# Rows of the value tile 144 bytes apart instead of 132, so that every row begins on 16 bytes

## Chip, cores and metric

One core of one Trainium2 chip. The metric is the device time of one execution in microseconds (us). Six executions of this kernel lay between 427.55 and 428.86 us, 0.3% apart, so the change discussed here is read mostly from the traces: the hardware's own record of when each instruction started.

## The reference

Grouped-query attention (8 batches, 16 query heads over 4 key/value heads, 384 positions, head size 64), followed by a feed-forward layer with a squared ReLU.

```python
def _attn_ref(q, k, v):                       # q [8,16,384,64], k and v [8,4,384,64]
    k = np.repeat(k, group, axis=1); v = np.repeat(v, group, axis=1)
    scores = scale * np.matmul(q, k.transpose(0, 1, 3, 2))
    attn = np.exp(scores - np.max(scores, axis=-1, keepdims=True))
    attn = attn / (np.sum(attn, axis=-1, keepdims=True) + 1e-09)
    return np.matmul(attn, v)

def _moe_ref(x, w_in, w_out):                 # x [3072,1024], w_in [1024,2048], w_out [2048,1024]
    h = np.maximum(x @ w_in, 0.0)
    return h * h @ w_out
```

## The kernel before

The kernel keeps both weight matrices in on-chip memory (SBUF) and interleaves, on the tensor engine (PE), the attention of one batch with the feed-forward matmuls of an earlier one. Only one piece of it matters here. The values of a batch lie in a tile `v_aug` of 12 rows per partition (4 heads x 3 blocks of 128 positions). A row holds 64 values and a 1.0, so that one matmul gives both the weighted sum and the denominator of the softmax. It reads 65 of the 66 elements of a row: 130 of 132 bytes.

```python
    DP = D + 2                                                     # 66
    v_st  = [sb(f"v_st{i}", [128, NU, D]) for i in range(NST)]     # NU = 12 rows
    v_aug = [sb(f"v_aug{i}", [128, NU, DP]) for i in range(2)]     # batches take turns
    ...
    def aug_v(b, eng):                                             # on POOL
        R.add(eng, lambda e: e.tensor_copy(v_aug[b % 2][:, :, 0:D], v_st[b % NST][:, :, :]), ...)
    ...
    def av(b, c, banks):
        g, s2 = c // 2, c % 2
        i = pick(banks)
        po = bank(i)[:, 0:2 * NJ * DP].rearrange("p (f e) -> p f e", f=2 * NJ)
        def mm(pe, f0):
            for f in range(f0, f0 + NJ):
                for j in range(NJ):                                # NJ = 3 rows are accumulated
                    w = expT[:, (b * NU + g * NJ + j) % NEX, f % 2, (f // 2) * 128:(f // 2) * 128 + 128]
                    m = pe.matmul(po[:, f - 6 * s2, 0:D + 1], w, v_aug[b % 2][:, g * NJ + j, 0:D + 1],
                                  start=(j == 0), stop=(j == NJ - 1))
            return m
    ...                                        # reciprocal of column D, multiply, store as bf16
    for i in range(2):
        R.add("vector", lambda e, i=i: e.memset(v_aug[i][:, :, D:D + 1], 1.0), writes=[("v_one", i)])
```

So within a head `g` the matmuls read rows 3g, 3g+1, 3g+2, then jump back to 3g, 3g+1, 3g+2 and so on, six times per `av`. In all there are 1,152 such matmuls, mostly in bursts of 36. Each is preceded by its own weight load (1,152 LDWEIGHTS on the same line in the page below).

The softmax here doesn't subtract the row's maximum and nothing guards it: scores larger than these inputs give would overflow.

Of the kernel before, what the change touches and what calls it, by code (L numbers as in the profile page):

```python
# [139 lines left out]
def bass_gqa_attention__then__ffn_squared_relu_kernel(  # L140
# [11 lines left out]
    B, H, S, D = 8, 16, 384, 64  # L152
# [6 lines left out]
    NU = HKV * NJ  # L159
    UC = 4 * S  # L160
    HC = UC // 2
    DP = D + 2
    NST, NEX, NXT, NHR, NY = 2, 8, 3, 4, 3

    R = Recorder(nc)
# [1 line left out]
    def sb(name, shape, dt=bf16):  # L167
        return nc.alloc_sbuf_tensor(name, shape, dt)
# [5 lines left out]
    q_f32 = sb("q_f32", [128, 4, NJ * D], f32)  # L174
    k_dup = [sb(f"k_dup{i}", [128, NU, 2, D]) for i in range(2)]
    v_st = [sb(f"v_st{i}", [128, NU, D]) for i in range(NST)]
    v_aug = [sb(f"v_aug{i}", [128, NU, DP]) for i in range(2)]
    kT = [sb(f"kT{i}", [128, NU, 128]) for i in range(2)]
    qT = [sb(f"qT{i}", [128, 2 * NU, 128]) for i in range(2)]
    expT = sb("expT", [128, NEX, 2, HC])  # L180
# [11 lines left out]
    def bank(i):  # L192
        return ps[:, i, :]
# [4 lines left out]
    def pick(allowed):  # L198
        turn_count[0] += 1
        i = min(allowed, key=lambda i: (max(R.when(writes=[("bank", i)]), R.clock["tensor"]), used[i]))  # L200
        used[i] = turn_count[0]
        return i
# [171 lines left out]
# [5 lines that stand above are left out]
# [387 lines left out]
```

## Time and profile before

| | before |
|---|---|
| time, median | 427.7 us (427.55 to 427.76, 3 runs) |
| span of the profiled run | 426.2 us |
| PE busy | 420.4 us, 99% |
| the 1,152 attention-times-value matmuls on the chain that ended last | 8.3% of the span |
| their mean start to start, inside bursts | 31.2 ns |

The page of the kernel before: first the busy time of each engine, then the chain of work that ended last (share of the span by engine), then the two groups of line 383, PE matmuls and weight loads (busy us, mean ns of one, then idle time of the engine just before them).

```profile
PE 420.4 (99%) x3435; PEld 232.0 (54%) x3464; DVE 157.9 (37%) x332; ACT 194.8 (46%) x194; POOL 55.4 (13%) x68
...
PE 96%; DMA 1%; issue 1%; ACT 1%; POOL 1%; DVE 0%; POOLq 0%
...
L383 PEld LDWEIGHTS ps<-v_aug,expT 128*128 128x128 bf16 x1152 | 40.0, 97 | 6.9 <-issue 0.6
L383 PE MATMUL ps<-v_aug,expT 128*128 128x65 bf16 x1152 | 42.0, 193 | 0.0
```

PE is the bound, and it is bound by its own stream of matmuls, not by waits. Who PE waited for, in the same kernel (total us, times, longest):

```profile
PE ps L555 <- PEq L751: 0.8, 1, 0.8
PE ps L496 <- issue: 0.5, 3, 0.2
PE ps L311 <- DMA q_st<-in_q_dram: 0.4, 1, 0.4
PE ps L337 <- ACT expT L347: 0.2, 1, 0.2
```

These sum to 1.9 us. The mean of 193 ns in the group is the length of one record, whose end the profiler models; the records overlap, since their starts lie 31.2 ns apart. What counts is the distance between starts, called the interval or pitch below. The timeline of the kernel before shows it for three bursts (start us, length us, engine, line, how many):

```profile
240.28 1.26 PE L383 MATMUL ps<-v_aug,expT 128*128 128x65 bf16 x36
251.34 1.28 PE L383 MATMUL ps<-v_aug,expT 128*128 128x65 bf16 x36
257.87 1.28 PE L383 MATMUL ps<-v_aug,expT 128*128 128x65 bf16 x36
```

A burst of 1.28 us is 35 intervals and one length of 0.193 us: (1.28 - 0.193)/35 = 31.1 ns. The individual records give each interval to the nanosecond. Two bursts' beginnings, batch 5 (rows 0, 1, 2) and batch 4 (rows 3, 4, 5), in ns from each start to the next:

```
batch 5, rows 0 1 2:  29 35 32 | 30 32 33 | 29 33 33 | 29 32 33 | 29 32 32 | 29 34 32
batch 4, rows 3 4 5:  29 29 36 | 29 29 34 | 29 29 33 | 30 29 33 | 29 29 34 | 29 29 33
```

An interval is counted to the row read by the matmul at whose start it begins. It differs by row.

### The profile page before, as it was taken

How to read it: one execution, taken by the hardware profiler on the slowest of the kernel's cores; microseconds unless marked ns; L12 is line 12 of the kernel's file. 1: busy time of each engine (PE TensorE's matmuls, PEld its weight loads, DVE VectorE, ACT ScalarE, POOL GpSimd, SP SyncE). 2: the span in 40 equal slices, each digit the busy share in tenths (PEclk: the TensorE clock that was granted, in tenths of full speed). 3: DMA queues.
4: the chain of work that ended last, by engine and by line, in shares of the span. 5: the costliest groups of instructions: out<-in, count | busy, mean ns of one | idle time of the engine just before them, and what ended most of it. 6: DMA issues, size and time to landing. Idle time of an engine off the chain costs nothing.

```text
span 426.2 us, 7813 instructions
## 1 busy us (share of the span) xinstructions
PE 420.4 (99%) x3435; PEld 232.0 (54%) x3464; DVE 157.9 (37%) x332; ACT 194.8 (46%) x194; POOL 55.4 (13%) x68
## 2 busy tenths in 40 slices
PE   8999999999999999999999999999999999999997
PEld 6565554555545555455554455544564465446544
DVE  3664431343424443144442344422441244114412
ACT  6957730477355773547745377552240033003300
POOL 8680001234013004003100000000000000000000
DMA  9999999999789178938918321033001100110012
GB/s 177 184 184 200 186 201 226 180 158 158 145 182 167 26 106 125 149 94 134 120 45 180 92 34 25 12 88 102 25 2 49 74 26 2 49 74 26 1 67 82
DMA packets 96915, 44.30 MB, mean 104 GB/s; under 512 B 77296, under 2 KB 90864, under 8 KB 96880
## 3 DMA queue, kind: packets, MB, share of 16 engines
q0 software_dynamic: 36544, 17.44, 32.1%
q1 hardware_dynamic: 59664, 25.86, 28.7%
q8 instruction: 27, 0.44, 0.4%
q10 hardware_dynamic: 672, 0.49, 0.4%
q14 instruction: 8, 0.07, 0.1%
HBM read 35.65 MB, written 12.58 MB: 113 GB/s over the span
## 4 chain that ended last, share of the span: by engine, by line
PE 96%; DMA 1%; issue 1%; ACT 1%; POOL 1%; DVE 0%; POOLq 0%
PE ps L440 40%; PE ps L496 39%; PE ps L383 8%; PE ps L358 7%; DMA q_st<-in_q_dram 1%; PE ps L337 1%; ACT expT L347 1%; PE ps L311 0%; PE ps L416 0%; POOL q_st L239 0%; PE ps L294 0%; POOL v_st L232 0%; DVE qT L318 0%; DVE y_sb L505 0%; POOL ident L523 0%
## 5 line engine op out<-in xcount | busy, mean ns | idle before, releaser
L440 PE MATMUL ps<-xT,w_in_sb 128*128 128x384 bf16 x1024 | 174.8, 326 | 0.0
L496 PE MATMUL ps<-w_out_sb,h2T 128*128 128x512 bf16 (+2 forms) x755 | 167.5, 375 | 1.9 <-issue 0.5
L368 ACT ACTIVATE expT<-ps 128x3072 bf16<-128x3072 f32 x42 | 114.5, 2727 | 64.8 <-PE ps L358 64.0
L440 PEld LDWEIGHTS ps<-xT,w_in_sb 128*128 128x128 bf16 x1024 | 97.0, 98 | 69.6 <-issue 6.8
L450 ACT ACTIVATE h2T<-hr 128x384 bf16<-128x384 f32 x128 | 64.5, 520 | 140.9 <-DVE hr L448 140.9
L496 PEld LDWEIGHTS ps<-w_out_sb,h2T 128*128 128x128 bf16 x784 | 73.8, 98 | 87.1 <-issue 5.1
L448 DVE TENSOR_SCALAR hr<-ps 128x384 f32<-128x384 f32 x128 | 71.2, 557 | 106.4 <-PE ps L440 106.4
L505 DVE COPY y_sb<-ps 128x512 f32<-128x512 f32 (+2 forms) x49 | 33.4, 681 | 122.8 <-PE ps L496 122.8
L383 PEld LDWEIGHTS ps<-v_aug,expT 128*128 128x128 bf16 x1152 | 40.0, 97 | 6.9 <-issue 0.6
L383 PE MATMUL ps<-v_aug,expT 128*128 128x65 bf16 x1152 | 42.0, 193 | 0.0
L398 DVE TENSOR_TENSOR o_sb<-ps,rinv 128x384 bf16<-128x384 f32 x64 | 35.7, 558 | 2.2
L358 PE MATMUL ps<-qT,kT 64*128 64x512 bf16 (+1 forms) x336 | 34.6, 325 | 0.0
L358 PEld LDWEIGHTS ps<-qT,kT 64*128 64x128 bf16 x336 | 13.0, 94 | 20.7 <-issue 6.3
L392 DVE RECIPROCAL rinv<-ps 128x6 f32<-128x6 f32 x64 | 12.2, 190 | 27.3 <-PE ps L383 27.3
L271 POOL COPY v_aug<-v_st 128x768 bf16<-128x768 bf16 x8 | 6.6, 831 | 83.9 <-PE ps L383 68.4
L347 ACT ACTIVATE expT<-ps 128x1024 bf16<-128x1024 f32 (+1 forms) x20 | 16.9, 980 | 1.1 <-PE ps L337 0.8
L266 POOL COPY k_dup<-k_st 128x1536 bf16<-128x1536 bf16 x7 | 10.3, 1470 | 43.5 <-DMA k_st<-in_k_dram 43.5
L239 POOL DMA_DIRECT2D q_st<-in_q_dram x17 | 14.8, 883 | 0.9 <-POOLq L751 0.8
L207 POOL DMA_DIRECT2D k_st<-in_k_dram x7 | 5.3, 757 | 39.4 <-DMA qT<-q_st 39.4
L337 PE MATMUL ps<-qT,kT 64*128 64x384 bf16 (+2 forms) x48 | 7.5, 343 | 0.3 <-ACT expT L347 0.2
L249 POOL DMA_DIRECT2D w_in_sb<-in_moe_w_in_dram x8 | 7.1, 891 | 0.0
L232 POOL DMA_DIRECT2D v_st<-in_v_dram x8 | 6.3, 784 | 0.1
(26 smaller groups left out, 41.9 us busy)
## 6 DMA issues: line engine op xcount, KB each, us to landing
out_dram<-y_sb SPq DMA_DIRECT2D x47, 256.0 KB, 2.0
q_st<-in_q_dram POOLq DMA_DIRECT2D x14, 384.0 KB, 8.2
w_in_sb<-in_moe_w_in_dram POOLq DMA_DIRECT2D x8, 512.0 KB, 14.5
w_out_sb<-in_moe_w_out_dram POOLq DMA_DIRECT2D x4, 1024.0 KB, 30.8
v_st<-in_v_dram POOLq DMA_DIRECT2D x8, 192.0 KB, 9.8
k_st<-in_k_dram POOLq DMA_DIRECT2D x7, 192.0 KB, 4.4
q_st<-in_q_dram POOLq DMA_DIRECT2D x3, 192.0 KB, 5.4
xT<-o_sb SPq DMA_TRANSPOSE x28, 3.1
```

Of the source, the lines that this page charges most:

```text
L239: R.add("gpsimd", lambda g: g.dma_start(q_st[st][:, h0:h1, :], q[b, h0:h1].rearrange("h (p j) d -> p h (j d)", j=NJ)), writes=[("q_st", st ...
L347: R.add("scalar", lambda e: e.activation(dst, src, AF.Exp, scale=0.125), reads=keys, writes=[("expT", (b * NU + u) % NEX, t) for u, _, _ i ...
L358: m = pe.matmul(flat[:, k0 * HC + c0:k0 * HC + c1], kT[b % 2][64 * x:64 * x + 64, u + k0, :], q_cols(b, (u + k0) // NJ, x, c0, c1))
L368: R.add("scalar", lambda e: e.activation(dst, src, AF.Exp, scale=0.125), reads=keys, writes=[("expT", (n + m) % NEX, t) for m in range(2) ...
L383: m = pe.matmul(po[:, f - 6 * s2, 0:D + 1], w, v_aug[b % 2][:, g * NJ + j, 0:D + 1], start=(j == 0), stop=(j == NJ - 1))
L392: R.add("vector", lambda e: e.reciprocal(rinv[r].ap().unsqueeze(2), po[:, :, D:D + 1]), reads=[("bank", i)], writes=[("rinv", r)], cost=0.13)
L398: R.add("vector", lambda e: e.tensor_tensor(dst, srcv, rbv, ALU.mult), reads=[("bank", i), ("rinv", r)], writes=[("o_sb", o, s2)], cost=0.48)
L440: m = pe.matmul(bank(i)[:, 0:S], w_in_sb[:, kc, c * 128:(c + 1) * 128], xT[b % NXT][:, kc, :], start=(kc == 0), stop=(kc == NKC - 1))
L448: R.add("vector", lambda e: e.tensor_scalar_max(hr[r][:, :], bank(i)[:, 0:S], 0.0), reads=[("bank", i)], writes=[("hr", r)], cost=0.48)
L450: R.add("scalar", lambda e: e.activation(h2T[b % 2][:, c, :], hr[r][:, :], AF.Square), reads=[("hr", r)], writes=[("h2T", b % 2, c)], cost ...
L496: m = pe.matmul(bank(i)[:, 0:n], h2T[b % 2][:, c, i3 * 128:(i3 + 1) * 128], w_out_sb[:, c, c0:c1], start=(c == 0), stop=(c == NFC - 1))
L505: R.add("vector", lambda e: e.tensor_copy(ysl, bank(i)[:, 0:n]), reads=[("bank", i)], writes=[("y", yb)], cost=0.08 + n / 960)
```

## The change

The intent: with rows 132 bytes apart, three rows in four begin off a multiple of 16 bytes. At 144 bytes every row begins on one.

```diff
-    DP = D + 2
+    DP, DV = D + 2, D + 8
@@
-    v_aug = [sb(f"v_aug{i}", [128, NU, DP]) for i in range(2)]
+    v_aug = [sb(f"v_aug{i}", [128, NU, DV]) for i in range(2)]
```

The layout (`DP`) in PSUM, the memory that matmuls write into, stays. Both value tiles start on 64 bytes before and after, and all later tensors move by 256 bytes. The order of instructions on every engine is the same in both kernels.

## The prediction

> **What bounds the kernel.** The tensor engine. Busy row of the page: PE 420.4 us of a span of 426.2 (99%). The chain of waits that ended last is 96% PE; its attention-times-value matmuls (line 383, 128x65) hold 8%, about 35 us. The wait table gives PE 1.9 us of idle.
>
> **What the change does.** Same instructions, order and PSUM layout. Value rows start 144 instead of 132 bytes apart, so all start on 16 bytes. Before, both value tiles start on a multiple of 64 bytes and take 1,600 with padding; they will take 1,728, so later tensors move by 256 bytes and keep their alignment. Only the value copy on POOL (8 x 831 ns, off the chain), two 68 ns fills, and the 1,152 matmuls see the new spacing.
>
> **Cost, read from the single matmul records.** Start to start inside the bursts is 31.2 ns on average, but depends on the row that is read. Rows 0 and 8: 29.2. Rows 1, 2, 5, 7, 10, 11: 31.9 to 33.6. Row 4 (16-aligned): 29.2. But misalignment itself costs nothing: rows 3 and 9 (offsets 12 and 4 within 16 bytes) run at 29.5 and 29.1, and rows 3, 6 and 9 take 29 straight after a feed-forward matmul. What slow rows share is the junction: the last of the 65 elements of the row before lies in the 16-byte piece in which the new row starts. Where a row starts on 16 bytes, or the matmul jumps back two rows, the piece is another and the pitch is 29. The exception is row 6 after row 8: 31.3 although the pieces differ; there row 8's last piece holds a single element.
>
> [...] this trace shows 29.2 in the fast cases, 162.8 for 384 columns.
>
> After the change no junction shares a line. Best: all 1,152 at 29.2, saving 1,152 x 2.0 ns = 2.3 us. Against it: every row then ends with one element alone in its line, like row 8. If a third of the matmuls (the jumps back) then cost 31.3, the mean is 29.9 and the gain 1.5 us; if all do, nothing is gained. PE almost never waits, so nearly all reaches the end; in the first 26 us, where exp on ACT paces PE, up to 0.3 us may be lost.
>
> **Predicted:** 425.8 us (-0.4%), 8 in 10 between 425.0 and 427.4. Faster by over 2%: 0.01; within 2%: 0.98; slower: 0.01. 2% would be 8.6 us, or 7.4 ns of each 31.2: out of reach.
>
> **What would show it.** Right: pitch of slow rows 1, 2, 5, 7, 10, 11 falls to about 29; the 36-matmul bursts shrink from 1.28 us to about 1.21 in the timeline; PE idle stays near 2 us. Wrong: if jumps or all rows sit at 31 to 33, the single-element line is what costs; if PE idle grows by what the bursts lose, the gain was off the path; if feed-forward pitches change, another tensor's address mattered.
>
> **What would make it wrong.** A cost that belongs to a row's own place in memory, or to accumulation, rather than to junctions.

427.7 us before, less 1.9, is 425.8. The 1.9 lies midway between the gains of 2.3 and 1.5 us that the text weighs, and both come from intervals of the trace of before (31.2 in the mean, 29.2 at best, 31.3 for row 6). By a "line" the text means a piece of 16 bytes. Its 0.3 us at the start are an estimate; 144 matmuls of batch 0 at 2.0 ns come to as much. Of the exp on ACT there, the trace of before shows 20 activations without a break from 5.88 to 23.09 us; PE waited for them once, for 0.2 us.

## The result

| | before | after |
|---|---|---|
| time, median | 427.87 us (427.55 to 428.86, 6 runs) | 427.28 us (426.92 to 428.15, 6 runs) |
| ratio | | 0.9984, 95% interval 0.9970 to 0.9999 |
| span of the profiled run | 426.2 us | 425.1 us |
| mean start to start inside bursts | 31.22 ns | 30.54 ns |

A ratio here is the mean time of one kernel's fast runs over that of the other's of the same rounds, so it is not quite the ratio of the medians quoted. The gain is 0.6 us where 1.9 was forecast.

The page of the kernel after, the same four lines:

```profile
PE 419.2 (99%) x3435; PEld 231.1 (54%) x3464; DVE 157.7 (37%) x332; ACT 194.8 (46%) x194; POOL 55.3 (13%) x68
...
PE 96%; DMA 1%; issue 1%; ACT 1%; POOL 1%; DVE 0%; POOLq 0%
...
L383 PEld LDWEIGHTS ps<-v_aug,expT 128*128 128x128 bf16 x1152 | 39.3, 98 | 6.9 <-issue 0.6
L383 PE MATMUL ps<-v_aug,expT 128*128 128x65 bf16 x1152 | 41.2, 193 | 0.0
```

and the same three bursts in its timeline:

```profile
239.35 1.26 PE L383 MATMUL ps<-v_aug,expT 128*128 128x65 bf16 x36
250.39 1.26 PE L383 MATMUL ps<-v_aug,expT 128*128 128x65 bf16 x36
256.90 1.26 PE L383 MATMUL ps<-v_aug,expT 128*128 128x65 bf16 x36
```

The bursts came to 1.26 us (the first took 1.26 before the change too), not to the 1.21 that was forecast. The busy time of these matmuls between 31 us and 294.3 us (seven of the eight batches) is a sharper measure, and it will serve for every experiment: start and end of the stretch, its length, PE busy (matmuls), PEld busy (weight loads), clock, DMA (share and GB/s). Before:

```profile
31.00:294.30 263.30, 35.76 (x1008) 34.95 (x1008) 1.00 0.78 126
```

After:

```profile
31.00:294.30 263.30, 35.09 (x1008) 34.32 (x1008) 1.00 0.78 125
```

So 0.67 us went from these 1,008 matmuls. Matching the weight loads of the two traces one by one gives the same: the changed kernel runs ahead by 0.43 us at 31 us and by 1.08 us when the last burst is over, and by 1.08 us at the end. The 0.65 us in between are the bursts. Nothing was lost on the way: PE takes what the bursts release. The feed-forward matmuls of 384 columns keep their interval (162.5 ns in both), and PE's waits after the change sum to 2.0 us, where they were 1.9:

```profile
PE ps L555 <- PEq L751: 0.8, 1, 0.8
PE ps L496 <- issue: 0.5, 3, 0.2
PE ps L311 <- DMA q_st<-in_q_dram: 0.3, 1, 0.3
PE ps L337 <- DVE qT L318: 0.2, 1, 0.2
PE ps L337 <- ACT expT L347: 0.2, 1, 0.2
```

The other 0.43 us are not the change's. They arise in the first 12 us, where PE waits once for a load of queries, whose landing varies from run to run; the changed kernel traced again (e8 below) is level with before at 31 us. The start of the waiting matmuls shows the landing. The timeline of before, PE:

```profile
8.98 0.49 PE L311 MATMUL ps<-ident,q_st 128*128 128x128 bf16 x6 [0.44 <-DMA q_st<-in_q_dram]
```

of after:

```profile
8.58 0.49 PE L311 MATMUL ps<-ident,q_st 128*128 128x128 bf16 x6 [0.31 <-DMA q_st<-in_q_dram]
```

and of e10_rows128_order021 below, a kernel with the same loads in the same order:

```profile
9.83 0.49 PE L312 MATMUL ps<-ident,q_st 128*128 128x128 bf16 x6 [1.34 <-DMA q_st<-in_q_dram]
```

Measured at 31 us, the kernels lie from 0.45 us ahead of the trace of before to 0.83 us behind it. A single time, or a single span, therefore says nothing about an effect of 0.7 us.

And the intervals of the changed kernel look new. The same two bursts:

```
batch 5, rows 0 1 2:  29 35 29 | 29 29 35 | 30 29 29 | 35 29 29 | 29 30 35 | 29 29 29
batch 4, rows 3 4 5:  29 35 29 | 29 30 29 | 35 29 29 | 29 35 29 | 30 29 29 | 35 29 29
```

Most matmuls now take 29 ns, but every fourth or fifth takes 35 (241 of 1,115), whichever row it reads: the means by row lie between 30.0 and 31.4 ns. The mean comes to 30.5, not 29.2.

### The profile page after: what moved, and what is told of

Same layout as the page of the kernel before. It is cut to its first block, busy times and chain, and to the rows that moved or that the text cites. A ratio compares the mean times of both kernels' runs of the same rounds, so it can differ in the third digit from the quotient of the medians.

```text
span 425.1 us, 7813 instructions
## 1 busy us (share of the span) xinstructions
PE 419.2 (99%) x3435; PEld 231.1 (54%) x3464; DVE 157.7 (37%) x332; ACT 194.8 (46%) x194; POOL 55.3 (13%) x68
## 4 chain that ended last, share of the span: by engine, by line
PE 96%; DMA 1%; issue 1%; ACT 1%; POOL 1%; DVE 0%; POOLq 0%
PE ps L440 40%; PE ps L496 39%; PE ps L383 8%; PE ps L358 7%; DMA q_st<-in_q_dram 1%; PE ps L337 1%; ACT expT L347 1%; PE ps L311 0%; PE ps L416 0%; PE ps L294 0%; POOL q_st L239 0%; POOL v_st L232 0%; DVE qT L318 0%; DVE y_sb L505 0%; POOL ident L523 0%
## 5 line engine op out<-in xcount | busy, mean ns | idle before, releaser
L505 DVE COPY y_sb<-ps 128x512 f32<-128x512 f32 (+2 forms) x49 | 33.3, 681 | 122.6 <-PE ps L496 122.6
## 6 DMA issues: line engine op xcount, KB each, us to landing
w_out_sb<-in_moe_w_out_dram POOLq DMA_DIRECT2D x4, 1024.0 KB, 30.2
```

What stands on the lines that cost most here:

```text
L505: R.add("vector", lambda e: e.tensor_copy(ysl, bank(i)[:, 0:n]), reads=[("bank", i)], writes=[("y", yb)], cost=0.08 + n / 960)
```

## The experiments

Two questions. First, was the old cost at the junction of two rows that share a 16-byte piece (junction theory, as predicted), or at rows that begin off 16 bytes (alignment theory)? Second, why does the changed kernel not run at 29.2? Candidates: a last piece with a single element in it; a cost per 16-byte piece, of which a row covers nine; the weight load that goes with each matmul; or something in the count of columns. "Mean interval" below is that of batches 1 to 7 (981 intervals inside bursts; batch 0 runs in short pieces at the start). On this measure before has 31.13 ns and after 30.45. The experiments ran on three chips. The chip is not what differs: kernels with 65 columns at 144 bytes gave 30.45 on two of them (one batch of e4, and e8), and two with nothing shared gave 30.33 and 30.50 on the third (e10 and e9).

### e1_order021: the old layout, another order

```diff
-                for j in range(NJ):
+                for j in (0, 2, 1):
@@
-                                  start=(j == 0), stop=(j == NJ - 1))
+                                  start=(j == 0), stop=(j == 1))
```
(on the kernel before)

> Old 132-byte spacing, but each group of three accumulates rows in the order 0, 2, 1, so that no matmul starts in the 16-byte piece in which the one before ended. Right result. If the cost is in the shared piece (junction theory), the mean pitch inside the bursts falls from 31.2 ns to the 30.5 of the changed kernel, about 0.7 us in the span, with no byte of the layout changed. If it is in the misaligned row itself (alignment theory), the mean stays at 31.2 and the time at that of before.

Mean interval 30.29 ns. Busy time of the bursts, this kernel:

```profile
31.00:294.30 263.30, 34.91 (x1008) 34.13 (x1008) 1.00 0.79 126
```

That is 0.85 us below before and 0.18 us below the changed kernel. Time 426.96 us (426.77 to 427.57, 5 runs) against 427.80 of before (427.61 to 429.83, 10 runs), ratio 0.9980 (0.9967 to 0.9994). The result is correct. No byte of the layout moved, three rows in four still begin off 16 bytes, and the whole gain of the change is there. The alignment theory falls. The order as such is worth little: with rows 128 bytes apart and the new order (e10 below) the mean is 30.33 ns, against 30.45 of the changed kernel in the old order.

### e3_rows148: rows off 16 bytes, but no shared piece

```diff
-    DP, DV = D + 2, D + 8
+    DP, DV = D + 2, D + 10
```
(on the kernel after)

> Rows 148 bytes apart: starts at 0, 4, 8, 12 within 16 bytes as in the kernel before, but no two rows touch a common piece. Junction theory: as the changed kernel, mean pitch 30.5, 29 and 35 ns mixed without regard to the row. Alignment theory: as the kernel before, 31.2, with rows off 16 bytes at 32 to 34.

Mean interval 30.21 ns; correct. Busy time of the bursts:

```profile
31.00:294.30 263.30, 34.82 (x1008) 34.05 (x1008) 1.00 0.81 126
```

Rows that begin 0, 4, 8 and 12 bytes into a piece are as fast as aligned ones, even a little faster (34.82 against 35.09 us), when they share nothing. The detail of the expectation missed: the intervals are not the changed kernel's 29 and 35 without regard to the row, but 29 to 35 with a pattern by row. The mean is what the junction theory said.

### e5_rows128 and e10_rows128_order021: every row on 16 bytes, and every junction shared

```diff
-    v_aug = [sb(f"v_aug{i}", [128, NU, DV]) for i in range(2)]
+    v_aug = [sb(f"v_aug{i}", [128, NU + 2, D]) for i in range(2)]
+    v_flat = [t.ap().rearrange("p u d -> p (u d)") for t in v_aug]
@@
-        R.add(eng, lambda e: e.tensor_copy(v_aug[b % 2][:, :, 0:D], v_st[b % NST][:, :, :]),
+        R.add(eng, lambda e: e.tensor_copy(v_aug[b % 2][:, 0:NU, 0:D], v_st[b % NST][:, :, :]),
@@
-                    m = pe.matmul(po[:, f - 6 * s2, 0:D + 1], w, v_aug[b % 2][:, g * NJ + j, 0:D + 1],
+                    m = pe.matmul(po[:, f - 6 * s2, 0:D + 1], w, v_flat[b % 2][:, (g * NJ + j) * D:(g * NJ + j) * D + D + 1],
@@
-        R.add("vector", lambda e, i=i: e.memset(v_aug[i][:, :, D:D + 1], 1.0), writes=[("v_one", i)])
+        R.add("vector", lambda e, i=i: e.memset(v_aug[i][:, NU:NU + 2, :], 1.0), writes=[("v_one", i)])
```
(on the kernel after; the tenth kernel has the order 0, 2, 1 of the first experiment besides)

> Wrong result on purpose: rows 128 bytes apart, 65 columns read, so that the 65th column is the first element of the next row. Every row starts on 16 bytes, as in the changed kernel, and every row ends in the very piece in which the next one starts. Junction theory: slow, about 31.5 ns or more in the mean, the second and third matmul of each three at 32 to 34, the jumps back at 29. Alignment theory, and the pieces theory without a junction cost: 30.5 as in the changed kernel.

Mean interval 31.52 ns, slower than the kernel before. Busy time of the bursts (line numbers moved by one), rows 128 bytes apart in the order 0, 1, 2:

```profile
31.00:294.30 263.30, 36.14 (x1008) 35.30 (x1008) 1.00 0.80 126
```

Within each three, the jump back takes 29 and the other two 32 to 33, in every head alike. So beginning on 16 bytes does not help where the piece is shared.

> Wrong result on purpose: as the run with rows 128 bytes apart (31.5 ns), only the order within each three is 0, 2, 1, so that no matmul starts in the piece in which the one before ended. Every byte read is the same. Junction theory: the mean falls from 31.5 to about 30.4. If the 128-byte spacing itself were what was slow there, it stays at 31.5.

Mean interval 30.33 ns; rows 128 bytes apart in the order 0, 2, 1:

```profile
31.00:294.30 263.30, 34.98 (x1008) 34.22 (x1008) 1.00 0.81 126
```

The same bytes, the same addresses, another order: 1.16 us less. (The times, one look at each, are 428.15 and 428.11 us and hide this: at 31 us the tenth kernel is 1.1 us behind the fifth.) Together the four kernels fill the table:

| mean interval, ns | no piece shared | some or all shared |
|---|---|---|
| every row on 16 bytes | 30.45 (after), 30.33 (e10) | 31.52 (e5: 8 of 12 junctions) |
| rows off 16 bytes | 30.29 (e1), 30.21 (e3) | 31.13 (before: 6 of 12 junctions) |

Each shared junction costs (31.52 - 30.33) x 12/8 = 1.8 ns in the one pair and (31.13 - 30.29) x 12/6 = 1.7 ns in the other. Against the other kernels with nothing shared it comes to 1.4 to 2.0 ns. That is about half of what single intervals suggested (33 against 29).

Two rivals can be checked in the trace of before. If starting close behind the end of the row before were what costs, every step to the next row would cost the same, since all of them start 2 bytes behind that end. If pieces of 8 bytes were what is shared, each head would have one shared junction. By pieces of 16 bytes, rows 0 to 2 and 9 to 11 have two shared junctions, the others one. The sums of the three intervals (batches 1 to 7) are 94.5 and 93.9 ns in the heads with two, 92.2 and 93.2 in those with one, and 91.2 to 91.5 in the changed kernel with none. They follow the count by 16 bytes.

### e9_rows160: no piece of 32 bytes shared either

```diff
-    DP, DV = D + 2, D + 8
+    DP, DV = D + 2, D + 16
```
(on the kernel after)

> Rows 160 bytes apart, 65 columns, right result: no two rows touch a common piece of 16 or of 32 bytes (at 144, every second junction shares a piece of 32). If the pieces that must not be shared are of 16 bytes, nothing changes: mean pitch in the batches after the first 30.4 to 30.5, with the 35s. If the 35s of the changed kernel come from sharing pieces of 32 bytes, they vanish and the mean falls to 30.0 or less.

Mean interval 30.50 ns, with the 35s of the changed kernel; correct. Busy time of the bursts:

```profile
31.00:294.30 263.30, 35.19 (x1008) 34.39 (x1008) 1.00 0.79 125
```

At 144 bytes every second junction shares a 32-byte piece, here none, and nothing is gained: 16 bytes are enough, and the 35s have another cause. Time 427.01 us, one look.

### e2_cols66: two elements in the last piece

```diff
-                    m = pe.matmul(po[:, f - 6 * s2, 0:D + 1], w, v_aug[b % 2][:, g * NJ + j, 0:D + 1],
+                    m = pe.matmul(po[:, f - 6 * s2, 0:D + 2], w, v_aug[b % 2][:, g * NJ + j, 0:D + 2],
@@
-        R.add("vector", lambda e, i=i: e.memset(v_aug[i][:, :, D:D + 1], 1.0), writes=[("v_one", i)])
+        R.add("vector", lambda e, i=i: e.memset(v_aug[i][:, :, D:D + 2], 1.0), writes=[("v_one", i)])
```
(on the kernel after)

> New 144-byte spacing, 66 columns instead of 65 (a second ones column), so that the last 16-byte piece of a row holds two elements. Right result. In the changed kernel every fourth or fifth matmul takes 35 ns instead of 29. If the single element in the last piece causes that (single-element theory), the 35s vanish [...]: mean 29.7, about 1 us less than the changed kernel. If the matmuls are paced by something else at about 30.5 ns (nine pieces per row, or the weight load of each), the mean stays at 30.5 and the time that of the changed kernel.

Mean interval 30.45 ns, with 240 intervals of 35; correct. Time 427.28 us (426.93 to 427.86, 5 runs) against 427.80, ratio 0.9992 (0.9980 to 1.0005). Busy time of the bursts, beside 35.09 of the changed kernel:

```profile
31.00:294.30 263.30, 35.08 (x1008) 34.31 (x1008) 1.00 0.80 126
```

The single element is not the cause of the 35s. And 66 columns cost exactly what 65 cost: a hint that was worth following.

### e4_cols_sweep and e6_cols_sweep2: the price of a column

A different count of columns in each batch, all from the start of the row. Their outputs are wrong, which doesn't matter for the times.

```diff
+    COLS = ((0, 65), (0, 57), (0, 60), (0, 61), (0, 67), (0, 68), (0, 69), (0, 73))   # by batch
@@
-                    m = pe.matmul(po[:, f - 6 * s2, 0:D + 1], w, v_aug[b % 2][:, g * NJ + j, 0:D + 1],
+                    m = pe.matmul(po[:, f - 6 * s2, 0:COLS[b][1]], w, v_aug[b % 2][:, g * NJ + j, COLS[b][0]:sum(COLS[b])],
```
(e6, on the kernel after, with rows of 80 elements and as many in PSUM; all columns from 64 on are filled with 1.0. e4 is written alike, rows of 72 elements, with 65, 32, 48, 56, 64, 65, 66, 72 columns.)

The figures expected of e4 are estimates. They agree with 29.2 ns at 65 columns, read from the trace of before, and 0.417 ns for each column more or fewer: the same trace has intervals of 55.9 ns at 128 columns (line 496), 162.5 at 384 and 216.0 at 512, so (162.5 - 55.9)/256 = 0.416 and (216.0 - 162.5)/128 = 0.418. Those of e6 take 0.417 ns for a column too, and 2.4 ns besides, from e4 (25.9 ns at 56 columns, 29.1 at 64, 32.45 at 72). The 3.38 ns for each piece of 16 bytes in e6 (about 3.3 in e4) is the interval of 30.4 over nine pieces.

> Wrong result on purpose. New 144-byte spacing; the columns read per matmul differ by batch: 65, 32, 48, 56, 64, 65, 66, 72. If the weight load or the issue of the load-and-multiply pair paces the bursts, the mean pitch stays at about 30.4 ns for all of 32 to 66 columns. If pieces of 16 bytes pace them at about 3.3 ns each, 64 columns (8 pieces) run flat at 28.8 ns without any 35, 56 at about 25.5, 48 at 22, 32 at 15.5 or at another floor; 65 and 66 (9 pieces) average 30.4, and 72 runs flat at 32.1. If a single element in the last piece is what costs, 64, 66 and 72 are all flat (28.8, 29.6, 32.1) and only 65 shows 35s.

> Wrong result on purpose: rows 160 bytes apart, the columns read differ by batch: 65, 57, 60, 61, 67, 68, 69, 73. From the first sweep a matmul of N columns takes N/2.4 + 2.4 ns where nothing else holds it. Pieces theory (max of that and about 3.38 ns for each 16-byte piece touched): 57: 27.0, 60: 27.4, 61: 27.8, 65: 30.4, 67: 30.5, 68: 30.7, 69: 31.2, 73: 33.8. Theory of columns rounded up to a multiple of four (8 bytes): 57 and 60: 27.4, 61: 29.1, 67 and 68: 30.7, 69: 32.4, 73: 34.1. Nothing but columns: 57: 26.2, 61: 27.8, 69: 31.2, 73: 32.8.

Bursts of 36 matmuls with 32, 64, 65 and 66 columns in the timeline of e4:

```profile
36.83 1.06 PE L384 MATMUL ps<-v_aug,expT 128*128 128x32 bf16 x36
158.71 1.21 PE L384 MATMUL ps<-v_aug,expT 128*128 128x64 bf16 x36
194.66 1.26 PE L384 MATMUL ps<-v_aug,expT 128*128 128x65 bf16 x36
230.38 1.26 PE L384 MATMUL ps<-v_aug,expT 128*128 128x66 bf16 x36
```

Measured, mean interval of the batch in ns, beside a formula found afterwards, (N rounded up to even)/2.4 + 2.5. It is an estimate: 1/2.4 is the 0.417 ns for a column, and 2.5 is what is left of the 162.5 ns at 384 columns, or of the 55.9 at 128:

| columns N | 32 | 48 | 56 | 57 | 60 | 61 | 64 | 65 | 66 | 67 | 68 | 69 | 72 | 73 |
|---|---|---|---|---|---|---|---|---|---|---|---|---|---|---|
| measured | 25.3 | 25.3 | 25.9 | 26.7 | 27.5 | 28.3 | 29.1 | 30.45 | 30.4 | 31.1 | 31.1 | 31.6 | 32.45 | 33.8 |
| formula | 15.8 | 22.5 | 25.8 | 26.7 | 27.5 | 28.3 | 29.2 | 30.0 | 30.0 | 30.8 | 30.8 | 31.7 | 32.5 | 33.3 |
| long intervals (some 6 ns above the rest)? | no | no | no | no | no | no | no | yes | yes | yes | yes | no | no | yes |

Three things follow. The weight load is not the limit at 65 columns: pairs of load and matmul keep up 25.3 ns at 32 and at 48 columns. (The formula reaches 25.3 only at 54.7 columns, so it can hold from there on alone.) The pieces theory misses at 67 columns (31.1 measured against 30.5 expected). The rounding to multiples of four misses at 61 (28.3 against 29.1). What fits is a rounding up to even counts: 57 take 26.7 and 61 take 28.3, and 65 are paid as 66 (30.45 and 30.4). And 65 to 68 and 73 columns, alone, show the long intervals, and stand 0.3 to 0.5 ns above the formula. Columns read and columns written changed together here, so which side the rounding and the long intervals belong to is not shown.

### e7_start_sweep: the same columns over more pieces

```diff
-    COLS = ((0, 65), (0, 57), (0, 60), (0, 61), (0, 67), (0, 68), (0, 69), (0, 73))
+    COLS = ((0, 65), (0, 64), (4, 64), (1, 64), (4, 60), (4, 61), (7, 57), (7, 58))
```
(on e6; first column and count)

> Wrong result on purpose: rows 160 bytes apart; by batch (first column, columns): (0,65), (0,64), (4,64), (1,64), (4,60), (4,61), (7,57), (7,58). The same 64 columns touch 8 pieces of 16 bytes from column 0 and 9 from column 4 or 1; (4,60) ends just inside the eighth piece and (4,61) reaches into a ninth; (7,57) and (7,58) likewise. No two rows share a piece. Pieces theory: 29.1, then 30.4, 30.4 for (4,64) and (1,64); (4,60) 27.4 but (4,61) 30.4; (7,57) 27.0 but (7,58) 30.4. If only the count of columns matters, in any rounding: 64 columns 29.1 wherever they start, 60 and 61 within 1.7 of each other, 57 and 58 equal. If misalignment itself costs: all five that start off 16 bytes are slower than the same count from column 0, (4,60) and (7,57) included.

| first column, columns | 0, 64 | 4, 64 | 1, 64 | 4, 60 | 4, 61 | 7, 57 | 7, 58 |
|---|---|---|---|---|---|---|---|
| pieces of 16 bytes | 8 | 9 | 9 | 8 | 9 | 8 | 9 |
| measured, ns | 29.1 | 29.2 | 30.6 | 27.5 | 28.4 | 27.5 | 29.0 |

The pieces theory, which had seemed right after the first sweep, falls: 64 columns over nine pieces take 29.2 ns, as over eight, and 61 columns from column 4 take 28.4, not 30.4. A start 8 bytes into a piece costs nothing (27.5 at 60 columns both ways). A start on an odd element does cost: 64 columns from column 1 take 30.6, and 57 and 58 from column 7 take 27.5 and 29.0, where the formula for even starts gives 26.7 for both. In these three batches that is a cost of starting off 4 bytes, 0.8 to 2.3 ns. Counting the 4-byte words that a row touches would explain column 1 (33 words, as 66 columns: 30.4) but not column 7, where 29 and 30 words would give 26.7 and 27.5. In the kernel before and after all rows begin on 4 bytes.

### e8_after_again: the changed kernel once more

> The changed kernel once more, unaltered, on one chip with the runs above. The mean pitch inside the bursts should come out at 30.5 again with a 35 every fourth or fifth matmul. Time: 0.65 to 0.75 us below before (ratio 0.9983), plus or minus what the start of the kernel varies by, about 0.4 us in single traces.

Mean interval 30.45 ns again. Busy time of the bursts:

```profile
31.00:294.30 263.30, 35.09 (x1008) 34.31 (x1008) 1.00 0.80 126
```

Between 31 us and the end of the bursts the trace gains 0.65 us on that of before, again; at 31 us it is level with it. Time 427.62 us (427.33 to 428.74, 5 runs) against 428.17 (427.80 to 430.03, 10 runs), ratio 0.9997 (0.9983 to 1.0011). The medians differ by 0.55 us; the means of five runs cannot show it.

## Why the prediction was right or wrong

- **Right: what bounds the kernel, and that the bursts' gain reaches the end.** 0.65 us gained in the bursts are 0.65 us gained at the end, in two traces. PE's waits stayed near 2 us (1.9 before, 2.0 and 2.3 in the two traces of the changed kernel).
- **Right: the cause of the old cost.** It is the shared 16-byte piece, not the misaligned row. The reordering alone removes it (31.13 to 30.29) and sharing brings it back on aligned rows (31.52). The change helps because 144 bytes leave no junction shared; the 16-byte starts are incidental (148 bytes: 30.21).
- **Wrong: the size, in the term "all 1,152 at 29.2, saving 1,152 x 2.0 ns = 2.3 us" and its milder form of 29.9.** The saving per matmul is 0.68 ns (31.22 to 30.54), so 1,152 x 0.68 = 0.8 us, of which the traces show 0.65 in seven of eight batches. The 29.2 ns were read from single intervals of the kernel before, and it never held them for three matmuls in a row: inside a burst, at most two intervals of 30 ns or less follow each other. So the step that failed is the floor that was assumed for matmuls without a shared junction: 29.2 ns, where the changed kernel runs at 30.5. The sums of three were there to be read: in the heads with only one shared junction they came to 29.5 + 29.2 + 33.5 = 92.2 ns (rows 3, 4, 5) and 31.2 + 32.8 + 29.2 = 93.2 (rows 6, 7, 8), or 30.7 and 31.1 per matmul, already close to the 30.45 that no sharing at all gives. It looks as if a short interval ahead of a long one is partly paid back by it: in the order 0, 2, 1 (e1), with nothing shared, each three still has one interval of 32 to 33 beside two near 29. That would also be why a shared junction seemed to cost 4 ns and costs about 1.7. This reading is argued from the patterns; no run isolates it.
- **Wrong: what was taken to confirm the floor.** What the trace of before gives itself, 65/2.4 + 2.5 = 29.6 ns, is an estimate from its intervals at 128 and 384 columns. The runs show 65 paid as 66, which gives 30.0. The remaining 0.45 ns go with the 35s. A row of 65 bf16 elements reached 30.2 ns at best in any layout tried.
- **Wrong: the counterweight.** The fear was a single element alone in the last piece. With two there nothing changes (30.45). What the row 6 exception was (31.3 after row 8) is not explained; with the changed layout row 6 has 31.4 ns again, the highest mean of any row (the other rows that follow a jump back have 31.2, 30.5 and 30.2).
- **Open:** what makes the long intervals at 65 to 68 and 73 columns and not at 64, 69 or 72. It is not the weight load, the single element, the count of 16-byte pieces, or sharing of 32-byte pieces. Nor is it the spacing of the results in PSUM: at 66 and at 72 elements (e8 and e4) 65 columns take 30.45 ns alike. It is worth at most 0.45 ns x 1,152 = 0.5 us here.

No version beats the changed kernel clearly: the old layout in the order 0, 2, 1 does as well, at no cost in memory.

## What to carry to other kernels

Short matmuls that follow one another should not begin in the 16-byte piece in which the one before ended: here, at 65 bf16 columns, each such junction cost about 1.7 ns of some 31. A different order of the accumulation cured that as well as padding did (30.29 ns against 30.45), and padding to 16 bytes for its own sake brought nothing (30.45 at 144 bytes, 30.21 at 148). A saving per instruction must be taken from sums over a whole repeating group, not from the short intervals among them, since short intervals may come only together with long ones. And before a gain is forecast for a group, ask what the stage would cost with the suspected part gone: here a sweep of the column count gave that floor in one run.
